# The 512 by 512 channel layer by seven block products, top bits of late weights on another engine, and a new table of the order

## The chip, the cores and the metric

One NeuronCore of one Trainium2 chip runs the whole program as one launch. The metric is device time in microseconds; before the change it is 362.84 us, the median of 3 runs (362.77 to 362.84).

## What is computed

The reference is a retention layer, a spectral mixing layer with a channel layer, and a gated MLP, all in float32. Cut to what matters here:

```python
# retention: B, H, S, D = 2, 8, 768, 64
state = gamma * state + einsum('bhd,bhe->bhde', k[:, :, t], v[:, :, t])
y[:, :, t] = scale * einsum('bhd,bhde->bhe', q[:, :, t], state)
# mixing: d_model = 512
theta = x @ w_theta
y = einsum('ts,bsd->btd', w_tok_r, x * cos(theta)) + einsum('ts,bsd->btd', w_tok_i, x * sin(theta))
u = x + y
x = u + maximum(u @ w_ch, 0.0)
# gated MLP
h = gelu(x @ w_in)                      # 512 -> 1024, halves u and v
v_s = einsum('ts,bsd->btd', w_sg, layernorm(v) * g_ln) + b_sg
out = x + (u * v_s) @ w_out
```

The part in question is `u @ w_ch`: 1536 tokens (2 batches of 768), 512 channels in, 512 out.

## The kernel before

All matrix products are done to float32 precision with three matmuls each. An operand is split into a rounded high half (ScalarE, `split_hi`, line 339) and the rest as a low half (VectorE, `split_lo`, line 345), and `terms3` issues high x high, low x high and high x low. Activations lie with channels on the partitions: `x_tile(g, d)` is channel tile d (of 4) of token group g, 512 tokens wide. Groups 0 and 1 are the first 512 tokens of the two batches, group 2 (`B` in the code) takes the last 256 of both.

The program runs in this order: retention in 12 chunks (`scores`, `outer`, `attend`; masks and decays by VectorE and ScalarE), the angle `theta` of each chunk in two halves, each with its own half of the theta weights, the token mixing (`mix_main` for groups 0 and 1, `mix_rest` for group 2), the channel layer (`channels`, line 902), the up projection (`up_v`, `up_u`, `up_four`), the gate (`gate_tile`) and the last projection (`finish`, `finish_four`). The mixing ends in `mix_main`'s additions, each followed by `split_x`, which makes the high and low halves `uhl` that the channel layer reads.

A layer (`layer`, line 880) for one output tile of one group is 12 matmuls of 128x512: four input tiles, three terms. `seven` does it for four output tiles at a time (two groups, two tiles, all in blocks) with seven block products of 6 matmuls where eight would be the plain way: it needs sums of weight blocks (`sum_weights`) and of token tiles (`sum_tokens`), splits of these sums, and additions behind the products (`both`, and what its callers add). Before the change the up projection's first half (`up_four`) and the last projection (`finish_four`) use it; the channel layer does not.

Weights come as 64-bit words, 1024 to a partition, into one of two raw buffers (`raw`; the theta weights and one more go into x's own memory), and are turned into float32 by three steps: ScalarE rescales the high words (line 411), VectorE shifts the top bits of the low words down (line 421), VectorE joins the two (line 431). Then come a split into halves (lines 339 and 345) and the products.

Every operation is noted in a list first (`plan.op`); the table `ORDER`, a list of operation numbers, then fixes the order in which each engine gets its own, and which buffer each one takes. Loads are issued by SP in that order too; a load that waits for a buffer holds up all that is behind it on SP. Each engine runs its queue in order. PSUM has 8 banks of 512 words.

The lines the change touches: `weight` (line 421), `mix_main` (the splits at line 836), `channels` (902 to 913), `up_four` (1237 to 1251), the loop that calls `channels` (1353 to 1356) and `ORDER`.

```python
def split_x(res, g, d, prio, eng=dve):
    res[g, d] = pair()
    split(res[g, d], lambda: x_tile(g, d), 512, prio, x_keys(g, d), eng)
```

Of the kernel before, what the change touches and what calls it, by code (L numbers as in the profile page):

```python
# [10 lines left out]
F32 = mybir.dt.float32  # L11
F32R = mybir.dt.float32r
I32 = mybir.dt.int32
AF = mybir.ActivationFunctionType
ALU = mybir.AluOpType

B, H, S, D = 2, 8, 768, 64
# [21 lines left out]
RAWS, PAIRS, ONES = 2, 36, 7  # L39

TURNED = (0, 1)


class Buf:
# [21 lines left out]
class Plan:  # L66
# [105 lines left out]


ORDER = [
# [52 lines left out]
]  # L227


# [1 line left out]
def retention_spectral_gmlp(  # L231
# [154 lines left out]
    def weight(k, prio, eng=dve, after=()):  # L386
# [19 lines left out]
        def words(hi):  # L406
# [9 lines left out]
            r=[raw],  # L416
            w=[(raw, 1)],
        )
        dve(
            1024,  # L420
            lambda: V.tensor_scalar(  # L421
                out=words(0), in0=words(0), scalar1=29, scalar2=None, op0=ALU.logical_shift_right
            ),
            fast=True,
            prio=prio,
            r=[raw],
            w=[(raw, 0)],
        )
        dve(
            1024,  # L430
            lambda: V.scalar_tensor_tensor(  # L431
# [379 lines left out]
    def mix_main(b, s, prio):  # L811
# [14 lines left out]
        if s == NCH - 1:  # L826
            for d in range(NP):

                def add(d=d):
                    V.tensor_tensor(  # L830
                        out=x_tile(b, d), in0=ap(y[b, d]), in1=x_tile(b, d), op=ALU.add
                    )

                t = prio + 1 + d * 0.1
                dve(512, add, ps=True, r=[y[b, d]], w=x_keys(b, d), prio=t)
                split_x(uhl, b, d, t + 1 + LATE * (1 - b))

    def mix_rest(b, s, prio):
        i = b * NCH + s
# [59 lines left out]

    x2hl = {}  # L900

    def channels(g, e, prio):

        t = layer(W_CH, uhl, g, e, prio)

        def relu():
            u = x_tile(g, e)
            V.scalar_tensor_tensor(  # L908
                out=u, in0=ap(t), scalar=0.0, in1=u, op0=ALU.max, op1=ALU.add
            )  # L910

        dve(512, relu, ps=True, r=[t], w=x_keys(g, e), prio=prio)
        split_x(x2hl, g, e, prio)

    def gelu(t, o, prio, ps=True):

# [318 lines left out]
        dma(256, put, r=[o], prio=prio)  # L1235

    def up_four(j, ws, ts, prio):
        z, x, y, u, v = seven(W_INU, x2hl, ws, ts, j, prio)
        for g, f, part in ((0, j, z), (1, j, x), (0, 2 + j, y), (1, 2 + j, v)):
            if f % 2 == 0:  # L1240
                gu[g, f], gu[g, f + 1] = halves()
            t = part
            if part is not z:
                t = v if part is v else Buf()
                dve(
                    512,
                    lambda t=t, part=part: V.tensor_tensor(
                        out=ap(t), in0=ap(part), in1=ap(u), op=ALU.add
                    ),
                    ps=part is not v, r=[part, u], w=[t], prio=prio,  # L1250
                )
            gelu(t, gu[g, f], prio, ps=part is z)

    def finish_four(j, ws, ts, prio):
        z, x, y, u, v = seven(W_OUT, ghl, ws, ts, j, prio)
# [94 lines left out]
    for k in range(2):  # L1350
        weight(W_INU + k, t - 10 + 5 * k)
        weight(W_INV + k, t + 30 + 5 * k)
    for g in range(3):
        for e in range(NP):
            channels(g, e, t)
            t += 2.7
    ws = sum_weights(W_INU, t - 8)
    ts = sum_tokens(lambda g, d: (lambda: x_tile(g, d), x_keys(g, d)), t - 4)
    for f in range(NP):
# [144 lines left out]
```

## Time and profile before

| | |
|---|---|
| median of 3 runs | 362.84 us |
| the profiled execution, time | 362.86 us |
| the profiled execution, span | 361.1 us |
| TensorE matmul, busy | 356.1 us (99%), 2308 instructions |
| TensorE weight load, busy | 305.0 us (84%) |
| VectorE, busy | 295.5 us (82%), 476 instructions |
| ScalarE, busy | 187.0 us (52%), 314 instructions |
| GpSimd, busy | 9.0 us (3%) |
| moved by DMA | 44.33 MB |

The span goes from the first to the last instruction; the time of an execution is what the device reports around it. Busy times count from an instruction's start to its end: matmuls overlap each other, and so do the ends and starts of neighbours on VectorE and ScalarE, so that the distance from one start to the next is shorter than a busy time. In the rows PE is TensorE's matmuls, PEld its weight loads, DVE VectorE, ACT ScalarE, SPq the queue on SyncE that issues loads.

### The profile page before, as it was taken

To read this page: it belongs to the slowest core of one execution; us is meant where nothing else is said; L and a number is where in the kernel's file an instruction comes from. 1 tells how busy PE (TensorE), PEld (TensorE's weight loads), DVE (VectorE), ACT (ScalarE), POOL (GpSimd) and SP (SyncE) were. 2 spreads that over 40 slices of the span, in tenths; PEclk is the share of its full clock that TensorE was granted. 3 is DMA by queue.
4 is the path that set the end of the run, shared out by engine and by line. 5 is a ranking of instruction groups with operands and counts; after the bars stand their busy time and mean duration, and the time that the engine had idled before them with its cause. 6 is when DMAs were issued, how large, how long until landed. Compare 5 with 4: busy or idle time off the path is not lost.

```text
span 361.1 us, 5762 instructions
## 1 busy us (share of the span) xinstructions
PE 356.1 (99%) x2308; PEld 305.0 (84%) x2308; DVE 295.5 (82%) x476; ACT 187.0 (52%) x314; POOL 9.0 (3%) x18
## 2 busy tenths in 40 slices
PE   8999999999999999999999999999999999999996
PEld 8878888888999888889988888888888889988885
DVE  2799989899478798952788788799899979989984
ACT  1689895545255458524532365465588651342310
POOL 1110000010001000002000000000000000000000
DMA  7999675435773155056023000011000000000224
GB/s 297 416 408 414 259 238 214 182 116 175 239 269 141 54 193 159 0 218 235 0 118 116 0 2 0 0 30 60 0 0 3 0 1 2 2 0 0 72 104 174
DMA packets 13946, 44.33 MB, mean 123 GB/s; under 512 B 1760, under 2 KB 5344, under 8 KB 11488
## 3 DMA queue, kind: packets, MB, share of 16 engines
q1 hardware_dynamic: 13776, 43.92, 33.2%
q8 instruction: 18, 0.29, 0.3%
q14 instruction: 8, 0.07, 0.1%
q10 hardware_dynamic: 144, 0.05, 0.1%
HBM read 38.19 MB, written 5.77 MB: 122 GB/s over the span
## 4 chain that ended last, share of the span: by engine, by line
PE 93%; DMA 4%; DVE 1%; ACT 1%; issue 0%
PE banks L319 93%; DMA xb<-wts 3%; DMA dec<-decays 1%; DVE xb L431 0%; DVE b L345 0%; ACT xb L411 0%; ACT b L339 0%; PE banks L760 0%; DVE b L1311 0%
## 5 line engine op out<-in xcount | busy, mean ns | idle before, releaser
L319 PE MATMUL banks<-b,b 128*128 128x512 f32 (+2 forms) x1764 | 323.0, 350 | 0.5 <-DVE b L345 0.5
L319 PEld LDWEIGHTS banks<-b,b 128*128 128x128 f32 (+1 forms) x1764 | 274.2, 183 | 47.3 <-issue 1.9
L339 ACT ACTIVATE b<-b 128x512 fp32r<-128x512 f32 (+1 forms) x83 | 63.4, 788 | 72.0 <-PE banks L319 26.4
L345 DVE TENSOR_TENSOR b<-b,b 128x512 fp32r<-128x512 f32 (+1 forms) x83 | 70.8, 873 | 14.4 <-ACT b L339 8.9
L345 DVE TENSOR_TENSOR b<-xa,b 128x512 fp32r<-128x512 f32 (+1 forms) x26 | 18.5, 726 | 10.2 <-ACT b L339 10.2
L339 ACT ACTIVATE b<-xa 128x512 fp32r<-128x512 f32 (+1 forms) x26 | 16.9, 663 | 14.0 <-DVE xa L908 5.6
L511 DVE TENSOR_TENSOR b<-banks,causal 128x512 f32<-128x512 f32 x24 | 16.2, 684 | 7.1 <-PE banks L319 7.1
L411 ACT ACTIVATE b<-b 128x1024 f32<-128x1024 f32 x16 | 18.2, 1149 | 5.0 <-DMA b<-wts 4.9
L431 DVE SCALAR_TENSOR_TENSOR b<-b 128x1024 int32<-128x1024 int32 x16 | 19.7, 1228 | 1.2 <-ACT b L411 0.9
L319 PE MATMUL banks<-b 64*128 64x128 f32 (+1 forms) x352 | 19.4, 256 | 0.2
L319 PEld LDWEIGHTS banks<-b 64*128 64x128 f32 (+1 forms) x352 | 17.3, 165 | 2.2 <-DMA b<-qkv 0.8
L938 ACT ACTIVATE b<-b 128x512 f32<-128x512 f32 x24 | 14.6, 627 | 6.7 <-DVE b L928 6.7
L534 ACT ACTIVATE b<-b,dec 128x64 f32<-128x64 f32 x56 | 14.1, 335 | 6.4 <-DMA b<-qkv 6.4
L920 ACT ACTIVATE b<-banks 128x512 f32<-128x512 f32 x18 | 10.2, 589 | 9.3 <-PE banks L319 9.1
L928 DVE SCALAR_TENSOR_TENSOR b<-b,banks 128x512 f32<-128x512 f32 x18 | 12.1, 678 | 2.1 <-ACT b L920 1.9
L421 DVE TENSOR_SCALAR b<-b 128x1024 int32<-128x1024 int32 x16 | 11.0, 686 | 3.2 <-DMA b<-wts 3.2
L339 ACT ACTIVATE b<-xb 128x512 fp32r<-128x512 f32 (+1 forms) x13 | 8.4, 665 | 9.5 <-DVE xb L866 7.8
L782 DVE TENSOR_TENSOR b<-b,b 128x512 f32<-128x512 f32 x20 | 13.2, 680 | 0.1
L716 ACT ACTIVATE b<-banks 128x512 int32<-128x512 f32 x12 | 7.1, 589 | 11.8 <-PE banks L319 11.8
L1029 ACT ACTIVATE b<-b,rstd 128x512 f32<-128x512 f32 x12 | 9.6, 806 | 5.7 <-DVE rstd L1018 5.7
L944 DVE SCALAR_TENSOR_TENSOR b<-b,banks 128x512 f32<-128x512 f32 x18 | 11.9, 679 | 0.6 <-ACT b L938 0.4
L1202 ACT ACTIVATE b<-banks 128x512 f32<-128x512 f32 x8 | 4.7, 593 | 14.2 <-PE banks L319 13.0
(75 smaller groups left out, 217.6 us busy)
## 6 DMA issues: line engine op xcount, KB each, us to landing
b<-wts SPq DMA_DIRECT2D x16, 1024.0 KB, 5.1
b<-qkv SPq DMA_DIRECT2D x24, 512.0 KB, 9.7
out<-b SPq DMA_DIRECT2D x11, 256.0 KB, 2.1
scr<-b SPq DMA_DIRECT2D x5, 512.0 KB, 4.6
b<-scr SPq DMA_DIRECT2D x20, 128.0 KB, 3.1
b<-wsg SPq DMA_DIRECT2D x9, 256.0 KB, 7.4
xa<-wts SPq DMA_DIRECT2D x2, 1024.0 KB, 11.9
xb<-wts SPq DMA_DIRECT2D x1, 1024.0 KB, 10.6
```

The lines of the kernel that those rows point to most:

```text
L319: nc.tensor.matmul(out=o, lhsT=l, rhs=r, start=start, stop=stop, skip_group_check=more)
L339: act(words, lambda: A.activation(out=hi(), in_=src(), func=AF.Copy), prio=prio, r=r, **k)
L345: lambda: E.tensor_tensor(out=lo(), in0=src(), in1=hi().bitcast(F32), op=ALU.subtract),
L411: lambda: A.activation(out=words(1).bitcast(F32), in_=words(1).bitcast(F32), func=AF.Prelu, scale=REBIAS, alpha=SIGN_UP,),
L421: lambda: V.tensor_scalar(out=words(0), in0=words(0), scalar1=29, scalar2=None, op0=ALU.logical_shift_right),
L431: lambda: V.scalar_tensor_tensor(out=words(0), in0=words(1), scalar=3, in1=words(0), op0=ALU.logical_shift_left, op1=ALU.bitwise_or,),
L511: V.tensor_tensor(out=ap(at[i])[:, h * 512 + lo : h * 512 + hi].rearrange("p (n t) -> p n t", n=n), in0=ap(sc[h])[:, lo:hi].rearrange("p ( ...
L534: A.activation(out=v, in_=v, func=AF.Copy, scale=dk[:, h : h + 1])
L782: V.tensor_tensor(out=v, in0=x, in1=v, op=ALU.mult)
L928: lambda: V.scalar_tensor_tensor(out=ap(s), in0=ap(s), scalar=1.0 / GA, in1=ap(t), op0=ALU.add, op1=ALU.mult),
L938: lambda: A.activation(out=ap(s), in_=ap(s), func=AF.Tanh, scale=GA * GC),
L944: lambda: V.scalar_tensor_tensor(out=ap(o), in0=ap(s), scalar=1.0, in1=ap(t), op0=ALU.add, op1=ALU.mult),
```

## The change

1. The channel layer for groups 0 and 1 goes by `seven` (new `channels_four`, twice) in place of eight calls of `channels`; group 2 keeps its four layers. The additions behind the products are shared with `up_four` (new `sums_of`).
2. `mix_main` no longer splits tiles 0 and 1 of group 1, which the block products don't read.
3. For weights 8 to 18 (all but theta's and the main mixing weights) ScalarE makes the top bits of the low words, in place of VectorE: it reads the top byte of each low word as a number, takes a 32nd of it less 31/64, and writes the rounded whole number.
4. `ORDER` is another table.

```diff
+TOP_BY_ACT = range(W_REST, N_WP)
...
-    48, 50, 62, 49, 63, 105, 51, 106, 0, 52, 168, 118, 64, 53, 119, 55, 54, 56, 6, 67, 58, 57, 66,
+    50, 49, 48, 62, 63, 118, 105, 106, 51, 119, 55, 56, 0, 52, 57, 272, 64, 54, 53, 168, 67, 66, 58,
...
-        dve(
-            1024,
-            lambda: V.tensor_scalar(
-                out=words(0), in0=words(0), scalar1=29, scalar2=None, op0=ALU.logical_shift_right
-            ),
-            fast=True,
...
+        if k in TOP_BY_ACT:
+
+            def top():
+                b = home.bitcast(U8) if keys else ap(raw, I32).bitcast(U8)
+                return b.rearrange("p (n b) -> p n b", b=8)[:, :, 3]
+
+            act(
+                1024,
+                lambda: A.activation(
+                    out=words(0), in_=top(), func=AF.Copy, scale=1 / 32, bias=-31 / 64
+                ),
+                prio=prio, r=[raw], w=[(raw, 0)],
+            )
+        else:
...
-                split_x(uhl, b, d, t + 1 + LATE * (1 - b))
+                if b == 0 or d >= 2:
+                    split_x(uhl, b, d, t + 1 + LATE * (1 - b))
...
+    def channels_four(j, ws, ts, prio):
+        for g, e, t, ps in sums_of(seven(W_CH, uhl, ws, ts, j, prio), j, prio):
+            relu(g, e, t, ps, prio)
+
+    def sums_of(parts, j, prio):
+
+        z, x, y, u, v = parts
+        yield 0, j, z, True
+        for g, e, part in ((1, j, x), (0, 2 + j, y), (1, 2 + j, v)):
+            t = v if part is v else Buf()
+            dve(
+                512,
+                lambda t=t, part=part: V.tensor_tensor(
+                    out=ap(t), in0=ap(part), in1=ap(u), op=ALU.add
+                ),
+                ps=part is not v, r=[part, u], w=[t], prio=prio,
+            )
+            yield g, e, t, False
...
-    for g in range(3):
-        for e in range(NP):
-            channels(g, e, t)
-            t += 2.7
+    ws = sum_weights(W_CH, t - 30)
+    ts = sum_tokens(lambda g, d: (lambda: x_tile(g, d), x_keys(g, d)), t)
+    for j in range(2):
+        channels_four(j, ws, ts, t)
+        t += 9.5
+    for e in range(NP):
+        channels(B, e, t)
+        t += 2.7
```

The new table moves instructions on every engine. First the loads on SP, from the fifth on. Before (L400 is a weight's load: `xb` takes the first theta weight, `xa1` the second; L465 are the q/k/v loads of the chunks, two each; L490 is the query decay table):

```order
L465 DMA b4_111<-qkv 128x1024
L490 DMA dq_86<-qdecays 128x512
L465 DMA b5_114<-qkv 128x1024
L400 DMA xb_90<-wts 128x2048
L465 DMA b8_128<-qkv 128x1024
L465 DMA b9_130<-qkv 128x1024
L465 DMA b13_142<-qkv 128x1024
L400 DMA xa1_89<-wts 128x2048
```

And now, from the fifth on as well (L406 is the weight's load, L485 the q/k/v loads, L510 the decay table):

```order
L485 DMA b4_111<-qkv 128x1024
L485 DMA b5_113<-qkv 128x1024
L485 DMA b6_115<-qkv 128x1024
L510 DMA dq_86<-qdecays 128x512
L485 DMA b7_118<-qkv 128x1024
L406 DMA xb_90<-wts 128x2048
L485 DMA b11_146<-qkv 128x1024
L485 DMA b15_159<-qkv 128x1024
L485 DMA b18_181<-qkv 128x1024
L485 DMA b22_199<-qkv 128x1024
L406 DMA xa1_89<-wts 128x2048
```

Both theta weights stand further back: eight q/k/v loads ahead of the first where there were six, twelve ahead of the second where there were nine.

Second, TensorE ahead of its first theta product. Before, from the second chunk's attend on (64x64 are outer products, 128x128 of one buffer are scores, 64x128 the parts of an attend, L760 the transpose of a chunk, 128x512 theta):

```order
L319 MATMUL banks_65<-b1_105,state1_67 64x128 x8
L319 MATMUL banks_65<-b16_176,b3_109 64x128 x8
L319 MATMUL banks_65<-b5_114 64x64 x8
L760 MATMUL banks_65<-ident_69,xa0_88 128x128 x4
L319 MATMUL banks_65<-b4_111,state0_66 64x128 x8
L319 MATMUL banks_65<-b22_200,b5_114 64x128 x8
L319 MATMUL banks_65<-b8_128 128x128 x8
L319 MATMUL banks_65<-b9_130 128x128 x8
L319 MATMUL banks_65<-b32_273,b23_202 128x512 x2
L319 MATMUL banks_65<-b35_284,b23_202 128x512
```

And now, from the third chunk's attend on:

```order
L325 MATMUL banks_65<-b5_113,state0_66 64x128 x8
L325 MATMUL banks_65<-b27_239,b6_115 64x128 x8
L325 MATMUL banks_65<-b7_118 64x64 x8
L325 MATMUL banks_65<-b4_111,state1_67 64x128 x8
L325 MATMUL banks_65<-b23_201,b7_118 64x128 x8
L325 MATMUL banks_65<-b11_146 128x128 x8
L325 MATMUL banks_65<-b15_159 128x128 x8
L325 MATMUL banks_65<-b18_181 128x128 x8
L325 MATMUL banks_65<-b40_328,b36_314 128x512 x2
L325 MATMUL banks_65<-b44_341,b36_314 128x512
```

The fourth chunk's outer product and attend and two more scores now stand ahead of the first theta product (b40 and b44 are the high and low half of the first theta weight), the transpose behind it; in all 7 scores, 4 outer products and 4 attends, where there were 5, 3 and 3.

Third, VectorE ahead of the first product of the up projection by sums (L927 is the relu, L1199 a token sum for the up projection, L1248 the combining addition behind two products, L351 a low half). The relu that opens the piece waits for the channel layer's last block product but one on TensorE, and the last row is read by the up projection's first product:

```order
L927 SCALAR_TENSOR_TENSOR xa0_88<-banks_65,xa0_88 128x512
L1199 TENSOR_TENSOR b295_2012<-xa0_88,b287_1965 128x512
L1248 TENSOR_TENSOR b290_1979<-banks_65,b290_1979 128x512
L351 TENSOR_TENSOR b280_1940<-b255_1794,b280_1940 128x512
L351 TENSOR_TENSOR b296_2014<-xa0_88,b296_2014 128x512
```

In the kernel before this place has a relu of group 2 and low halves (L908 relu, L345 low half):

```order
L908 SCALAR_TENSOR_TENSOR xb_90<-banks_65,xb_90 128x512
L345 TENSOR_TENSOR b288_2042<-b285_2035,b288_2042 128x512
L345 TENSOR_TENSOR b278_2006<-xa1_89,b278_2006 128x512
L345 TENSOR_TENSOR b296_2083<-b286_2038,b296_2083 128x512
L345 TENSOR_TENSOR b293_2065<-b292_2063,b293_2065 128x512
```

Five instructions stand in both; now two of them are additions that the sums need.

## Rows read from the trace of the kernel before

**Rows 1.** The page, part 1: busy time, share of the span, instructions.
```profile
PE 356.1 (99%) x2308; PEld 305.0 (84%) x2308; DVE 295.5 (82%) x476; ACT 187.0 (52%) x314; POOL 9.0 (3%) x18
```

**Rows 2.** The chain of work that ended last: start, length in us, what.
```profile
0.79 3.97 DMA dec<-decays
...
4.77 10.56 DMA xb<-wts
...
20.34 18.55 PE banks L319 x226
...
39.48 318.51 PE banks L319 x1840
...
358.01 0.42 DVE b L1311
```

**Rows 3.** Waits of PE: line, who was waited for, us, times, longest.
```profile
PE banks L319 <- DVE b L345: 0.5, 1, 0.5
```

**Rows 4.** Groups on PE from 184 to 295 us, shapes apart: count, busy, ns.
```profile
L319 PE MATMUL banks<-b,b 128*128 128x512 f32 x485 | 110.3, 389 | 0.0
L319 PE MATMUL banks<-b,b 128*128 128x256 f32 x12 | 1.6, 283 | 0.0
```

**Rows 5.** Windows: length; busy of PE, PEld, DVE, ACT, POOL; clock, DMA, GB/s.
```profile
5.00:30.00 25.00, 24.32 (x360) 20.53 (x361) 21.04 (x33) 17.46 (x51) 2.82 (x4) 1.00 1.02 414
...
80.00:220.00 140.00, 140.00 (x871) 121.79 (x870) 105.36 (x149) 65.33 (x92) 3.55 (x4) 1.00 0.36 125
220.00:345.00 125.00, 125.00 (x621) 106.48 (x620) 112.98 (x221) 66.57 (x112) 0.00 (x0) 1.00 0.04 13
...
184.00:295.00 111.00, 111.00 (x497) 92.17 (x496) 96.91 (x197) 63.71 (x108) 0.00 (x0) 1.00 0.08 27
```

**Rows 6.** Groups by line and shape on DVE and ACT: count, busy us, mean ns, idle before.
```profile
L345 DVE TENSOR_TENSOR b<-b,b 128x512 fp32r<-128x512 f32 x55 | 36.2, 685 | 2.8 <-ACT b L339 2.8
...
L421 DVE TENSOR_SCALAR b<-b 128x1024 int32<-128x1024 int32 x16 | 11.0, 686 | 3.2 <-DMA b<-wts 3.2
...
L339 ACT ACTIVATE b<-b 128x512 fp32r<-128x512 f32 x55 | 33.2, 627 | 51.5 <-PE banks L319 16.8 <-DVE b L1106 15.4 <-DVE b L1158 9.2
...
L411 ACT ACTIVATE b<-b 128x1024 f32<-128x1024 f32 x16 | 18.2, 1149 | 5.0 <-DMA b<-wts 4.9
```

**Rows 7.** DVE in order of time: start, length in us, what, idle before.
```profile
169.91 0.69 DVE L345 TENSOR_TENSOR b<-xa,b 128x512 fp32r<-128x512 f32 x1 [6.94 <-ACT b L339]
...
201.41 0.68 DVE L1158 TENSOR_TENSOR b<-xa,xa 128x512 f32<-128x512 f32 x1
202.01 0.68 DVE L908 SCALAR_TENSOR_TENSOR xa<-banks,xa 128x512 f32<-128x512 f32 x1
...
216.80 0.69 DVE L908 SCALAR_TENSOR_TENSOR xb<-banks,xb 128x512 f32<-128x512 f32 x1 [1.81 <-PE banks L319]
```

**Rows 8.** PE in order of time, first 31 us: start, length, what (equal names merged).
```profile
7.16 0.94 PE L319 MATMUL banks<-ident 128*128 128x128 f32 x6
8.03 0.69 PE L319 MATMUL banks<-b 128*64 128x64 f32 x16
8.54 1.14 PE L319 MATMUL banks<-b,b 128*64 128x128 f32 x16
9.76 1.78 PE L319 MATMUL banks<-b 64*128 64x128 f32 x32
11.46 1.09 PE L319 MATMUL banks<-b,state 64*64 64x128 f32 x16
...
13.41 0.71 PE L319 MATMUL banks<-b 128*64 128x64 f32 x16
14.05 0.66 PE L760 MATMUL banks<-ident,xa 128*128 128x128 f32 x4
14.64 1.09 PE L319 MATMUL banks<-b,state 64*64 64x128 f32 x16
...
30.65 5.73 PE L319 MATMUL banks<-b,b 128*128 128x512 f32 x24
```

**Rows 9.** ACT in order of time, the second theta weight's first step.
```profile
21.67 1.15 ACT L411 ACTIVATE xa<-xa 128x1024 f32<-128x1024 f32 x1
```

More of the change, by code (lines that the diff above doesn't have):

```diff
@@ L13 @@
 I32 = mybir.dt.int32
+U8 = mybir.dt.uint8
 AF = mybir.ActivationFunctionType
@@ L418, in weight @@
         )
-        dve(
-            1024,
-            lambda: V.tensor_scalar(
-                out=words(0), in0=words(0), scalar1=29, scalar2=None, op0=ALU.logical_shift_right
-            ),
-            fast=True,
[L425 to L428, printed above, removed]
+        if k in TOP_BY_ACT:
[11 more added lines that the diff above has]
+            dve(
+                1024,
+                lambda: V.tensor_scalar(
+                    out=words(0), in0=words(0), scalar1=29, scalar2=None, op0=ALU.logical_shift_right
+                ),
+                fast=True,
+                prio=prio,
+                r=[raw],
+                w=[(raw, 0)],
+            )
         dve(
@@ L900, in retention_spectral_gmlp, with relu @@
     x2hl = {}
-    def channels(g, e, prio):
[L904 to L909, printed above, removed]
-            )
-        dve(512, relu, ps=True, r=[t], w=x_keys(g, e), prio=prio)
-        split_x(x2hl, g, e, prio)
+    def relu(g, e, t, ps, prio):
+        u = x_tile(g, e)
+        dve(
+            512,
+            lambda: V.scalar_tensor_tensor(
+                out=u, in0=ap(t), scalar=0.0, in1=u, op0=ALU.max, op1=ALU.add
+            ),
+            ps=ps, r=[t], w=x_keys(g, e), prio=prio,
+        )
+        split_x(x2hl, g, e, prio)
+    def channels(g, e, prio):
+        relu(g, e, layer(W_CH, uhl, g, e, prio), True, prio)
+    def channels_four(j, ws, ts, prio):
[6 more added lines that the diff above has]
+            t = v if part is v else Buf()
+            dve(
+                512,
+                lambda t=t, part=part: V.tensor_tensor(
+                    out=ap(t), in0=ap(part), in1=ap(u), op=ALU.add
+                ),
+                ps=part is not v, r=[part, u], w=[t], prio=prio,
+            )
+            yield g, e, t, False
     def gelu(t, o, prio, ps=True):
@@ L1237, in up_four @@
     def up_four(j, ws, ts, prio):
-        z, x, y, u, v = seven(W_INU, x2hl, ws, ts, j, prio)
-        for g, f, part in ((0, j, z), (1, j, x), (0, 2 + j, y), (1, 2 + j, v)):
+        for g, f, t, ps in sums_of(seven(W_INU, x2hl, ws, ts, j, prio), j, prio):
             if f % 2 == 0:
                 gu[g, f], gu[g, f + 1] = halves()
[L1242 to L1252, printed above, removed]
+            gelu(t, gu[g, f], prio, ps=ps)
     def finish_four(j, ws, ts, prio):
```

106 rows, old and new, of the table ORDER are left out of this document.

## The prediction

> **What bounds the kernel now.** I read the busy shares first: TensorE is at work for 99% of the span, VectorE 82%, ScalarE 52% [rows 1]. Then the chain of waits [rows 2]: the first load of a theta weight lands at 15.33, its conversion ends at 20.34, and from there TensorE runs unbroken to 357.99; 0.42 us of VectorE and the last store end the span. Then what TensorE waited for [rows 3]: once in the work, 0.5 us, for the low part of that theta weight. So from 20.34 on TensorE has no gap, and whatever leaves its queue leaves the time, unless a wait takes its place. The profiled execution took 362.86 us, 1.76 more than its span; the median of the runs is 362.84, so a sum made against this execution carries over.
>
> **The products.** Eight layers of 12 matmuls (groups 0 and 1, four tiles each) go; two times seven products of 6 come: 96 less 84 is 12 matmuls of 128x512. Their price is the distance from start to start, not the 389 ns that one is in flight. From 184 to 295 us TensorE had no idle, with 485 matmuls of 512 columns and 12 of 256 [rows 4, 5]; the 12 counted as 6, that is 111.0/491 = 0.226 us each. 12 x 0.226 = **2.71 us** off, in the stretch without gaps. Products by sums are in that stretch already (the up projection's), at no other price.
>
> **VectorE and ScalarE.** For the channel layer VectorE gains 4 sums of weights and 8 of tokens, 12 low halves of those, 4 combining and 6 further additions, and loses 2 low halves (group 1's mixed tiles 0 and 1, which no product reads any more): 32 instructions of 512 words. Back to back these start 0.60 us apart (201.41, 202.01 [rows 7]): 19.2 us. It loses 11 top-bit shifts, busy for 686 ns as a 512-word instruction is for 685 [rows 6, 7], so 0.60 apart too: 6.6 us. Net 12.6 us more. ScalarE gains 10 rounded halves and 4 copies of 512 words at 0.63, and 11 top-bit instructions. No row has that form (bytes read eight apart, whole numbers written); nearest is the rescaling of the same words at 1.15 [rows 6], which I take; the ends are 0.63 and twice 1.15. Together 21.4 us, 15.7 to 34 with those ends.
>
> What hides it: from 80 to 220 us, where the channel layer, its weights and its inputs lie, VectorE is idle for 140.0 - 105.4 = 34.6 us and ScalarE for 74.7 [rows 5]. With 12.6 more and a stretch 2.7 shorter, VectorE keeps 19. If that cover were gone, each microsecond would be one on TensorE. The tightest place, by the VectorE rows of the order, is the first product of the up projection: behind the relu that is released by the channel layer's last product but one on TensorE stand, in all, five VectorE instructions (relu, two additions, two low halves), 5 x 0.60 and some 0.4 for handing over, 3.4 us, against one product and one layer on TensorE, 1.36 + 2.71 = 4.07. The kernel before has a queue of five there too (a relu at 216.80 and four low halves [rows 7]), ahead of a product of the same kind, and TensorE did not wait. So: 0. With one more ScalarE step each late weight is ready about 1 us later, and the load that waits for its buffer, with all that is queued behind it on SP, starts as much later; these weights are converted well ahead of their products, and the DMA engines are 36% busy there [rows 5]: 0 again.
>
> **The start.** The new table moves the loads. The first theta weight is issued behind eight q/k/v loads and the decay table, where it stood behind six and the table; the second behind twelve, where it stood behind nine. At 414 GB/s (the stretch from 5 to 30 us [rows 5]) a 512 KB load takes 1.27 us, so they land 2.5 and 3.8 us later: 17.9, and, counted from 21.67, when ScalarE took up the second one [rows 9], 25.5. The first one is converted 5.0 us after landing, as before: 22.9. Ahead of its first product TensorE now has 7 scores, 4 outer products and 4 attends. An outer product takes 0.51 (8.03 to 8.54), with a scores 1.70 (9.76 to 11.46), an attend 1.95, the first one 1.22 [rows 8]: 4 x 1.70 + 3 x 1.2 + 1.2 + 3 x 1.95 = 17.5. It begins when V of chunk 0 has been scaled: decays landed at 4.76 [rows 2], one VectorE instruction and the handing over, 5.7; the wait for the first masks costs some 0.5. So 23.7, behind the weight's 22.9: no idle here, where there was 0.5, and no filling products, where there were 0.87 us of them at 7.16. By 23.7 it has done two scores, an outer product and an attend more than by 20.34, and not yet the transpose (0.59) and two theta products (0.45): 2.4 + 0.5 + 1.95 - 1.04 = 3.8 us of work in 3.36 us. **0.4 us** gained. Ends: 1.4, if all idle and filling time goes; -1.3, if everything lands one load later.
>
> The second theta weight is needed after three products, an attend, an outer product and another product: 23.7 + 4.1 + 1.95 + 0.5 + 1.4 = 31.6. Ready: 25.5 + 5.0, with two other VectorE instructions in between that partly run beside ScalarE, 30.5 to 31.7. I take 0.1 us lost; the ends are 0 and the 4.2 of the second rival.
>
> **Sum:** 362.86 - 2.71 - 0.4 + 0.1 = 359.85; I forecast **359.8 us**.
>
> **Rivals.**
> *VectorE becomes the bound, no gain.* After 220 us it is busy for 113.0 of 125 us [rows 5], and its idle before consists of waits, which more instructions need not fill. If the 24 added instructions that hang on the mixed tiles (32 less the 8 for weight sums; 14.4 us) cannot start before the last of these tiles, they meet the stage from 184 to 220; if a fifth of them is not covered, that costs 2.9: 362.86 - 2.71 + 2.9 = 363.05. Against it: the one long idle, 6.9 us, lies just there, ending at 169.91 [rows 7], and four of the eight token sums need tiles 0 and 2 alone. The Trainium skill speaks for this rival: "Perfetto Trace Analysis", section "Identifying the Most-Contended Engine", says that matmul busy time is no measure of TensorE's headroom and that weight-load busy time should be taken. By that rule TensorE stands at 84%, level with VectorE, and taking out matmuls at VectorE's cost would bring nothing. The trace does not agree here: starts 0.226 us apart fill the 111.0 us without idle, though weight loads are busy for only 92.2 of them.
>
> *The second theta weight is late: slower.* If one more load comes in ahead of it (1.27), it lands at 26.8; if its conversion again takes 9.0 us among other work, as from 21.67 to the first product with it at 30.65 [rows 8, 9], it is ready at 35.8. TensorE then idles 4.2: 362.86 - 2.71 - 0.4 + 4.2 = 363.95. The time is longer than before once that idle exceeds 3.1. For it: VectorE is busy 21.0 of 25 us from 5 to 30 [rows 5], and has more masks to make there now. Against: nothing waited for those 9.0 us, so they were no minimum.
>
> *The change does not take the time out*, because small waits along a new order give it back piece by piece: 361 to 362.1 if up to 2 us of them come together, still faster. For it: VectorE's and ScalarE's queues are cut finer in the new order; against: the order before held 338 us with no wait.
>
> **How the numbers follow.** A measurement of this kernel can tell 0.2%, 0.7 us. The forecast, with the start's ends, 358.8 to 360.9: 0.68. Small waits: 0.15. VectorE, no gain: 0.10. Late weight: 0.07. So faster by over 0.2% has 0.83, the same 0.10, slower 0.07. The range goes from the start's better end, 358.8, to 361.9, in the upper part of the small waits, and leaves some 2 in 10 outside.
>
> **What would show it.** Right: 1104 matmuls of 512 columns, no idle of TensorE behind VectorE from 40 us to the end, its unbroken run from about 23 or 24 to about 355, VectorE some 13 us busier or more, ScalarE some 20, the byte-reading instruction at 1.1 to 1.2 us. Wrong: idle of TensorE behind VectorE at the sums of the channel layer or the up projection (first rival); idle between 31 and 36 us behind the second theta weight (second); many idles of some tenths (third); a product that waits for a weight whose load stood behind a buffer on SP.

## The result, and the profile after

The median of five runs is **359.66 us** (359.16 to 360.20), against 362.84 before: 0.9913 of it, 95% interval 0.9898 to 0.9927, so 3.18 us less. Run again later beside other kernels it took 359.51 us, 0.9910 (0.9897 to 0.9922). The profiled execution took 359.16, the fastest of its five.

The page of the changed kernel, busy time of each engine, answers to [rows 1]:

```profile
PE 352.4 (99%) x2298; PEld 302.7 (85%) x2298; DVE 306.1 (86%) x497; ACT 204.5 (57%) x339; POOL 9.5 (3%) x18
```

VectorE is busy 10.6 us more than before, ScalarE 17.5 more, TensorE 3.7 less. The chain that ended last answers to [rows 2] (start, length in us, what):

```profile
5.35 10.03 DMA b<-qkv
...
15.41 2.02 ACT b L554 x8
...
17.98 0.69 DVE b L351
18.67 0.60 DVE xa L650
19.27 0.61 DVE xb L441
...
22.44 1.24 DVE b L351
...
23.72 18.28 PE banks L325 x200
...
45.77 308.52 PE banks L325 x1762
...
354.31 0.42 DVE b L1341
```

In this chain TensorE's unbroken run begins at 23.72 and ends at 354.29, where it was 20.34 and 357.99. Ahead of it the chain no longer goes through the load of the first theta weight, but through a q/k/v load that landed at 15.38, ScalarE's work on it, and VectorE's queue: the first theta weight's shift (L441) waited behind other work. What TensorE waited for in the work, in all (line, releaser, us, times, longest), answers to [rows 3]:

```profile
PE banks L325 <- DVE b L531: 0.6, 1, 0.6
```

That is the first masks, at 8.6 us. The windows answer to [rows 5], with their columns:

```profile
5.00:30.00 25.00, 24.39 (x363) 21.05 (x361) 20.01 (x32) 14.96 (x41) 1.84 (x3) 1.00 1.02 412
80.00:220.00 140.00, 140.00 (x872) 121.84 (x871) 117.04 (x167) 82.61 (x117) 3.52 (x4) 1.00 0.25 91
184.00:295.00 111.00, 111.00 (x514) 92.92 (x513) 105.02 (x208) 72.97 (x119) 0.00 (x0) 1.00 0.10 38
220.00:345.00 125.00, 125.00 (x621) 106.47 (x620) 115.26 (x225) 67.58 (x113) 0.00 (x0) 1.00 0.08 27
```

From 80 to 345 us TensorE has no idle, as before; VectorE's idle from 80 to 220 went from 34.6 to 23.0 us. The groups of ScalarE by line and shape (count, busy us, mean ns, idle before) show the instruction that no row of before had, beside the one whose price it was given [rows 6]:

```profile
L417 ACT ACTIVATE b<-b 128x1024 f32<-128x1024 f32 x16 | 18.4, 1150 | 0.0
...
L433 ACT ACTIVATE b<-b 128x1024 int32<-128x1024 uint8 x11 | 12.5, 1135 | 0.0
```

And TensorE in order of time answers to [rows 8]:

```profile
3.96 2.01 PE L325 MATMUL banks<-ident 128*128 128x128 f32 x14
5.89 2.68 PE L325 MATMUL banks<-b 128*64 128x64 f32 x48
9.13 1.09 PE L325 MATMUL banks<-b,b 128*64 128x128 f32 x16 [0.56 <-DVE b L531]
...
20.02 2.98 PE L325 MATMUL banks<-b 64*128 64x128 f32 x48
22.93 4.71 PE L325 MATMUL banks<-b,b 128*128 128x512 f32 x18
```

The 14 filling matmuls stand ahead of everything; the first theta product begins at 22.93, and its 18 matmuls took 4.71 us (4.40 in experiment 8, without a wait): the low half of the weight came at 23.68.

### The profile page after: what moved, and what is told of

Same layout as the page of the kernel before. It is cut to its first block, busy times and chain, and to the rows that moved or that the text cites. A ratio compares the mean times of both kernels' runs of the same rounds, so it can differ in the third digit from the quotient of the medians.

```text
span 357.5 us, 5782 instructions
## 1 busy us (share of the span) xinstructions
PE 352.4 (99%) x2298; PEld 302.7 (85%) x2298; DVE 306.1 (86%) x497; ACT 204.5 (57%) x339; POOL 9.5 (3%) x18
## 4 chain that ended last, share of the span: by engine, by line
PE 92%; DMA 4%; DVE 1%; ACT 1%; issue 0%; SPq 0%; DVEq 0%
PE banks L325 92%; DMA b<-qkv 3%; DMA dec<-decays 1%; ACT b L554 1%; DVE b L351 1%; ACT b L345 0%; DVE xb L451 0%; PE banks L780 0%; DVE xb L441 0%; DVE xa L650 0%; DVE b L1341 0%; SPq L510 0%; DVEq L451 0%
## 5 line engine op out<-in xcount | busy, mean ns | idle before, releaser
L345 ACT ACTIVATE b<-b 128x512 fp32r<-128x512 f32 (+1 forms) x95 | 70.7, 766 | 55.0 <-DVE b L1199 16.0
L351 DVE TENSOR_TENSOR b<-b,b 128x512 fp32r<-128x512 f32 (+1 forms) x95 | 78.2, 842 | 4.2 <-ACT b L345 3.7
L345 ACT ACTIVATE b<-xa 128x512 fp32r<-128x512 f32 (+1 forms) x24 | 15.9, 670 | 9.7 <-DVE xa L927 3.6
L345 ACT ACTIVATE b<-xb 128x512 fp32r<-128x512 f32 (+1 forms) x13 | 8.5, 667 | 17.6 <-DVE xb L650 9.9
L351 DVE TENSOR_TENSOR b<-xa,b 128x512 fp32r<-128x512 f32 (+1 forms) x24 | 17.4, 727 | 0.8 <-ACT b L345 0.7
L802 DVE TENSOR_TENSOR b<-b,b 128x512 f32<-128x512 f32 x20 | 13.8, 703 | 4.3 <-ACT b L771 2.6
L1243 ACT ACTIVATE b<-banks 128x512 f32<-128x512 f32 x12 | 7.1, 591 | 10.6 <-PE banks L325 10.6
L961 ACT ACTIVATE b<-banks 128x512 f32<-128x512 f32 x18 | 10.1, 585 | 5.2 <-PE banks L325 4.5
L433 ACT ACTIVATE b<-b 128x1024 int32<-128x1024 uint8 x11 | 12.5, 1135 | 0.0
L850 DVE TENSOR_TENSOR xa<-banks,xa 128x512 f32<-128x512 f32 x8 | 5.5, 687 | 8.0 <-PE banks L325 8.0
L1140 DVE SCALAR_TENSOR_TENSOR b<-banks,gcol,brow 128x512 f32<-128x512 f32 x12 | 9.0, 747 | 3.5 <-PE banks L325 3.5
```

Of the source, the lines that this page charges most:

```text
L345: act(words, lambda: A.activation(out=hi(), in_=src(), func=AF.Copy), prio=prio, r=r, **k)
L351: lambda: E.tensor_tensor(out=lo(), in0=src(), in1=hi().bitcast(F32), op=ALU.subtract),
L433: lambda: A.activation(out=words(0), in_=top(), func=AF.Copy, scale=1 / 32, bias=-31 / 64),
L802: V.tensor_tensor(out=v, in0=x, in1=v, op=ALU.mult)
```

## The experiments

My theory: TensorE has no gap from about 23 us on, so the 12 matmuls are worth their distance, 2.7 us; the work added to VectorE and ScalarE is hidden, with under 1 us to spare at the tightest place; the rest is the start. The rivals were those of the prediction. Each experiment ran in up to 11 executions beside the kernel before, with its ratio against that.

### 1. The start alone

```diff
-    48, 50, 62, 49, 63, 105, 51, 106, 0, 52, 168, 118, ...
+    50, 49, 48, 62, 63, 118, 105, 106, 51, 119, 55, 56, 0, 52, ...
...
```

In the kernel before, the table begins with the changed kernel's first 25 us; in the stretch behind it I moved entries until none of the planned waits that this made was left.

> The kernel before with the start of the changed one: the first 25 us of the order are the change's (the theta weights' loads behind more q/k/v loads, the retention work ahead of theta as in the change), the eight layers and VectorE's top bits stay. Theory (products 2.7, start 0.4): 362.4. If the start is worth what the changed kernel's trace suggests (its time fell by 3.7 in the profiled execution, 2.7 of it for the products): 361.8 to 362.0, and the rest of the change then brings 2.2 to 2.4 on top. Rival (the start gave nothing, the products and small things all): 362.8.

Measured: 362.91 us (362.20 to 363.54), ratio 1.0001 (0.9992 to 1.0010). By itself the new start brought nothing. TensorE in order of time shows why that reading is not the whole of it:

```profile
3.95 2.87 PE L319 MATMUL banks<-ident 128*128 128x128 f32 x14
6.75 2.67 PE L319 MATMUL banks<-b 128*64 128x64 f32 x48
...
23.75 3.02 PE L319 MATMUL banks<-b,b 128*128 128x512 f32 x12
```

The same 14 filling matmuls that took 2.01 us in the changed kernel's profile took 2.87 here, and everything behind them stands 0.8 us later. In every trace such matmuls start 0.213 us apart at first; where they go on long enough, they start 0.112 apart from some moment on: at 4.6 us in the changed kernel's profiled execution, at 6.4 in this one. That moment differs from execution to execution, and experiments 5, 6, 9, 10 and 11 are about it.

### 2. Twelve matmuls more

```diff
+TIMES = {559: 2, 585: 2}
...
-        o.fn()
+        for _ in range(TIMES.get(number[o], 1)):
+            o.fn()
```

The first product of each seven of the channel layer is computed twice into the same bank (the second start overwrites the first).

> The changed kernel with the first product of each seven of the channel layer computed twice: 12 matmuls of 128x512 more, all else the same. Theory (TensorE without gaps bounds): 12 x 0.226 = 2.7 us more, 362.4. Rival (VectorE bounds this stage): VectorE's queue gets 1.36 us of rest twice, so 0 to 0.5 us more, 359.7 to 360.2.

Measured: 362.56 us (361.92 to 362.73), ratio 0.9990 (0.9981 to 0.9999): 2.90 more than the changed kernel's median. The chain of waits gives the price without the start's scatter. The last long piece of this kernel:

```profile
46.02 311.25 PE banks L328 x1774
```

against 308.52 with 1762 in the changed kernel: 12 matmuls, 2.73 us, 0.2275 each. TensorE bounds, VectorE does not. And the kernel with the product count of before and all else changed stands 0.20 us under before by the medians (0.04 to 0.7 by the interval of the ratio): that is what the start and everything other than the products brought.

### 3. Top bits by VectorE

```diff
-TOP_BY_ACT = range(W_REST, N_WP)
+TOP_BY_ACT = ()
```

> The changed kernel with the late weights' top bits by VectorE, as before: 11 shifts at 0.60 for 11 ScalarE instructions at 1.14. Theory (hidden beside TensorE): within 0.3 of the changed kernel, 359.4 to 360.0, VectorE busy 6 to 7.5 us more and ScalarE 12.5 less. Rival (VectorE has nothing left once the sums are added): each shift is 0.6 on TensorE where it falls among the sums, up to 6.6 more, 361 to 366.

Measured: 359.51 us (359.15 to 359.96), ratio 0.9910 (0.9897 to 0.9924): no difference from the changed kernel. Its page:

```profile
PE 352.5 (99%) x2298; PEld 302.8 (85%) x2298; DVE 312.8 (88%) x508; ACT 194.0 (54%) x328; POOL 9.6 (3%) x18
```

VectorE 6.7 us more, ScalarE 10.5 less (I expected 12.5: part of the 1.135 us runs beside a neighbour), and the last long piece of the chain is 308.51 us. So this part of the change is worth nothing by itself in this order, and VectorE at 88% still covers.

### 4. VectorE late at its tightest place

```diff
+TIMES = {648: 3, 635: 3}
```

(the same loop as in experiment 2; 648 is a difference of tokens, 635 a low half, both between a relu and the low half that the up projection's first product waits for).

> The changed kernel with two of VectorE's instructions ahead of the up projection's first product (a difference of tokens and a low half, between the relu at 199.5 and the low half that ends at 202.6) done three times: four instructions more, 2.4 us, in the one place called the tightest. In the changed kernel's trace the product begins 0.8 us after its last low half, and needs that half only from its third matmul, 0.45 later. Theory (slack there is 0.7 to 1.2, nothing else hides it): TensorE idles 1.2 to 1.7 us at 203 us and the time rises by as much, to 360.9 to 361.4. Rival (the 19 us of VectorE's idle hide it): 359.7.

Measured: 360.57 us (360.44 to 361.34), ratio 0.9946 (0.9934 to 0.9959): 0.9 above the changed kernel's median, 1.28 above it in the two profiled executions, whose starts agree (5.89 and 5.90). VectorE and TensorE in order of time, first of the changed kernel, then of this one:

```profile
199.49 0.69 DVE L927 SCALAR_TENSOR_TENSOR xa<-banks,xa 128x512 f32<-128x512 f32 x1 [0.23 <-PE banks L325]
200.09 0.68 DVE L1199 TENSOR_TENSOR b<-xa,b 128x512 f32<-128x512 f32 x1
...
201.89 0.69 DVE L351 TENSOR_TENSOR b<-xa,b 128x512 fp32r<-128x512 f32 x1
```

```profile
199.53 0.69 DVE L930 SCALAR_TENSOR_TENSOR xa<-banks,xa 128x512 f32<-128x512 f32 x1 [0.23 <-PE banks L328]
200.14 2.14 DVE L1202 TENSOR_TENSOR b<-xa,b 128x512 f32<-128x512 f32 x3
...
204.85 0.68 DVE L354 TENSOR_TENSOR b<-xa,b 128x512 fp32r<-128x512 f32 x1
```

```profile
205.58 6.64 PE L328 MATMUL banks<-b,b 128*128 128x512 f32 x28 [0.88 <-DVE b L354]
```

In the changed kernel the queue of five runs from 199.49 to 202.58 and the product begins at 203.37: 0.79 us to spare. The four instructions put the low half at 205.53, 2.95 later. TensorE had by then done five of the product's six matmuls; the sixth, not the third as I had written, is the one that needs this half, and it waited until 205.58. In the changed kernel it stands at 203.37 + 5 x 0.227 = 204.5, so the real room is 1.9 us, and 2.95 less 1.9 is the 1.0 by which the sixth start came late, 1.27 us after the fifth. So the place was named rightly and hides little: the 19 us of VectorE's idle that I counted over the stage don't help here.

### 5. Four filling products in place of seven

```diff
-                keep_warm(idle[0], int((gap - (0.1 if done < 9.0 else 0.5)) / 0.24))
+                keep_warm(idle[0], min(4, int((gap - (0.1 if done < 9.0 else 0.5)) / 0.24)))
```

> The changed kernel with 4 filling products in place of 7 ahead of the first outer product (8 matmuls in the trace, not 14). In the profiles so far TensorE's matmuls of 128x128 go from 0.213 to 0.112 us apart at 4.5 to 6.4 us, another time in each execution, and in the changed order all 14 stand ahead of the first work: it began at 5.89 where the step came at 4.6, and at 6.75 where it came at 6.4. Theory (this wait, up to 0.85 us in some executions, is in the changed kernel's time and makes its runs differ): median 0.2 to 0.6 below the changed kernel's, 359.1 to 359.5, highest less lowest run under 0.6 us. Rival (the runs differ for another reason, and the first outer product waits for its input all the same): 359.6 with the same spread of 1 us; or the clock rises later for lack of work, 360 or more.

Measured: 359.04 us (358.79 to 359.84), ratio 0.9901 (0.9885 to 0.9916). As the theory said for the median, but the spread did not shrink (1.05 us), and experiment 10, the same kernel, takes it back.

### 6. The start alone, four filling products

The edit of experiment 5 in the kernel of experiment 1.

> The first experiment (the kernel before with the start of the changed one) with 4 filling products in place of 7. Theory (the start saves about 0.4 us of idle and filling, which the 14 filling matmuls gave back in the executions where the clock rose late): 362.1 to 362.5, spread under 0.6. Rival (the new start is worth nothing by itself): 362.8 to 363.

Measured: 362.46 us (361.88 to 363.42), ratio 0.9990 (0.9982 to 0.9999): 0.4 us under before, with the theory. Its spread is 1.5 us.

### 7. and 12. The second theta weight one load later

Experiment 7 moves one entry of the table, the second theta weight's load (6), behind a q/k/v load (273), with no filling products after 20 us; experiment 12 has the edit of experiment 5 besides.

```diff
-    ... 121, 70, 6, 110, 71, 109, 273, 108, ...
+    ... 121, 70, 110, 71, 109, 273, 6, 108, ...
...
-            if done < WARM and gap > (0.4 if done < 9.0 else 0.8):
+            if done < 20.0 and gap > (0.4 if done < 9.0 else 0.8):
```

> The changed kernel with the second theta weight's load one q/k/v load later on SP (and no filling products after 20 us). In the changed kernel it landed at 25.6, its low half was made at 31.21, and the first product with it began at 31.57, 0.36 later. Theory (conversion takes what it took, 5.6 us from landing): landing 1.27 later, 26.9, low half at 32.5, TensorE idles 0.4 to 0.9 us at 31.6 to 32.5 and the time rises by as much, to 360.1 to 360.5. Rival (the second one of the prediction: conversion takes 9.0 us once it is late): 4.2 us idle, 363.9. Other rival (the products' high terms and other work cover it): 359.7.

> The seventh experiment (second theta weight one load later) with 4 filling products, so that TensorE comes to that weight at about 29.7 to 30 and not, as in the seventh's profiled execution, 0.7 later than in the changed kernel. Theory: low half at 32.4, needed at 31.2 (or 0.45 later at the third matmul): 0.7 to 1.2 us of idle there and 0.7 to 1.2 above the fifth experiment, 359.8 to 360.3. Rival (late by 4.2): 363. Other rival (covered): 359.1.

Measured: experiment 7 360.35 us (359.59 to 360.91), ratio 0.9927 (0.9915 to 0.9940). That lies in the range forecast, but the wait forecast for it is not in its trace: in its profiled execution the work began at 6.96 and TensorE came to that weight as late as the weight itself. So the trace tells nothing of this wait, and what put the median 0.7 above the changed kernel's is not shown. For experiment 12 it is 359.31 us (359.25 to 359.90), ratio 0.9909 (0.9895 to 0.9923). The trace of experiment 12 is the one to read; VectorE in order of time, first of the changed kernel, then of experiment 12:

```profile
26.31 0.69 DVE L441 TENSOR_SCALAR xa<-xa 128x1024 int32<-128x1024 int32 x1
...
29.98 1.23 DVE L351 TENSOR_TENSOR b<-xa,b 128x1024 fp32r<-128x1024 f32 x1
```

```profile
26.72 0.70 DVE L441 TENSOR_SCALAR xa<-xa 128x1024 int32<-128x1024 int32 x1 [0.88 <-DMA xa<-wts]
...
30.41 1.23 DVE L351 TENSOR_TENSOR b<-xa,b 128x1024 fp32r<-128x1024 f32 x1
```

ScalarE took the weight up at 25.64 and at 26.72, 1.08 later. The low half ended at 31.21 and at 31.64, only 0.43 later: in the changed kernel the shift had waited behind two masks, here VectorE was free. Landing to low half was 5.6 us there and 4.9 here, and TensorE lost 0.1 us at 31.7. My 0.7 to 1.2 missed, because I carried the 5.6 over; the prediction's rival with its 9.0 us is out.

### 8. The first theta weight's bits joined earlier

```diff
-    ... 73, 74, 124, 115, 127, 18, 1, 2, 60, 3, 182, ...
+    ... 73, 74, 124, 1, 2, 3, 115, 127, 18, 60, 182, ...
```

(1 to 3 are that weight's rescaling, shift and joining, 115 the scaling of chunk 2), with the edit of experiment 5.

> The fifth experiment (4 filling products) with the first theta weight's top bits and their joining ahead of the scaling of chunk 2 on VectorE, where they stood behind it. In the changed kernel the low half of that weight came at 23.7, 0.7 after the first product had begun, and TensorE idled 0.2 between its high and its low terms. Theory: that idle goes, 0.2 us below the fifth experiment. Rival (chunk 2 and those behind it come late instead, slack there is 0.75 to 1.25): the same as the fifth experiment or up to 0.5 above.

Measured: 359.09 us (358.84 to 359.71), ratio 0.9897 (0.9884 to 0.9911), the same as experiment 5. Its profile has the gain and a loss. The first 18 theta matmuls take 4.40, without the idle between high and low terms; but at 62.86 TensorE has waited for VectorE (first VectorE in the changed kernel, then VectorE and TensorE here):

```profile
60.63 0.69 DVE L802 TENSOR_TENSOR b<-b,b 128x512 f32<-128x512 f32 x1 [1.45 <-DMA b<-scr]
```

```profile
61.51 0.69 DVE L802 TENSOR_TENSOR b<-b,b 128x512 f32<-128x512 f32 x1 [2.69 <-DMA b<-scr]
62.12 1.88 DVE L650 TENSOR_TENSOR xa<-banks,dq 128x512 f32<-128x512 f32 x3
```

```profile
62.86 3.47 PE L325 MATMUL banks<-b,b 128*128 128x512 f32 x14 [0.61 <-DVE xa L650]
```

L802 needs chunk 2 back from its way through DRAM. That transfer landed 0.88 us later than in the changed kernel (1.53 later than in experiment 5), and behind the wait in VectorE's queue stood the scalings that TensorE needed. The rival's reason, that chunk 2 comes late because it is scaled later, is not what the trace shows: it was scaled 1.6 us later, but it was sent to DRAM (L694) and the last of it asked for again (L700) no later than in the changed kernel. SyncE's queue in order of time, first of the changed kernel, then of this one:

```profile
33.06 0.33 SPq L694 DMA_DIRECT2D scr<-b  x1
...
54.31 0.91 SPq L700 DMA_DIRECT2D b<-scr  x2
```

```profile
32.64 0.33 SPq L694 DMA_DIRECT2D scr<-b  x1
...
54.15 0.96 SPq L700 DMA_DIRECT2D b<-scr  x2
```

The median is in the rival's range. Why the transfer landed late is not shown, nor whether the edit brings it about: the profiled execution, 359.71, is the slowest of its four, and the other three took 358.84 to 359.28.

### 9., 10. and 11. The changed kernel again, and the filling products

Experiment 9 is the changed kernel unaltered, 10 the kernel of experiment 5, 11 the same edit with 2 in place of 4.

> The changed kernel once more, unaltered, on the same chip as the next three, for a direct comparison. Theory (its time moves with the moment at which the filling matmuls get faster): median 359.4 to 359.9, runs between 359.1 and 360.4.

> The fifth experiment (4 filling products in place of 7) once more, on the same chip as the changed kernel. Theory: 358.9 to 359.3, 0.3 to 0.7 below the changed kernel here. Rival (the 0.6 between them came from different chips or executions): no difference above 0.2.

> The changed kernel with 2 filling products in place of 7. TensorE then rests from some 4.8 us to the first outer product at 5.8, whose input is not there earlier. Theory (the fillers only fill): as with 4, 358.9 to 359.4. Rival (without work TensorE's matmuls get faster later): the first scores run at 0.2 us a pair as in the slow part, masks and attends later by 0.5 to 1.5, 359.5 to 360.5.

Measured: experiment 9 359.51 us (359.13 to 359.88); experiment 10 360.05 (358.83 to 361.33), ratio 0.9926 (0.9905 to 0.9946); experiment 11 359.57 (359.18 to 360.31), ratio 0.9914 (0.9901 to 0.9926). TensorE in order of time, of 9, 10 and 11 in turn:

```profile
3.95 3.09 PE L325 MATMUL banks<-ident 128*128 128x128 f32 x14
6.97 2.67 PE L325 MATMUL banks<-b 128*64 128x64 f32 x48
...
23.98 4.38 PE L325 MATMUL banks<-b,b 128*128 128x512 f32 x18
```

```profile
3.96 1.40 PE L325 MATMUL banks<-ident 128*128 128x128 f32 x8
5.61 2.82 PE L325 MATMUL banks<-b 128*64 128x64 f32 x48 [0.25 <-DVE b L549]
...
22.93 1.42 PE L325 MATMUL banks<-b,b 128*128 128x512 f32 x5
```

```profile
3.96 1.06 PE L325 MATMUL banks<-ident 128*128 128x128 f32 x4
5.66 4.29 PE L325 MATMUL banks<-b 128*64 128x64 f32 x48 [0.65 <-DVE b L549]
...
24.02 1.20 PE L325 MATMUL banks<-b,b 128*128 128x512 f32 x4
```

In experiment 9 the filling matmuls stayed 0.213 apart to the last, 6.7 us; work began at 6.97 and the first theta product at 23.98, 1.05 later than in the other execution of the same kernel. Some of that came back at once (the low half was there, no idle between high and low terms), and the profiled time was 359.88 against 359.16. From there on the two executions are alike, the last piece of the chain:

```profile
46.49 308.52 PE banks L325 x1762
```

In experiment 11 the matmuls of the outer products and scores went on at the wide distance until 9.2 us. Its work began at 5.66, before that of the changed kernel, but its first theta product at 24.02, as late as in experiment 9: the rival's course and time. Experiment 10 missed: its median is 0.54 above that of experiment 9 beside it, where the theory had it 0.3 to 0.7 below. Three of its six executions took 360.83 to 361.33; the profiled one was the fastest, so what they lost, and where, is not shown. (A late transfer as in experiment 8 is one candidate.) The ten executions of that kernel have a median of 359.28, the nine of the changed kernel 359.66, with intervals that overlap. I found no version that is shown to beat the changed kernel.

## Why the prediction was right, and where its sizes were off

The forecast was 359.8 us; the time is 359.66.

- **The products**, 2.71 us: measured 2.73 (experiment 2, chain). TensorE had no gap and every matmul counted at its distance. The first rival, VectorE as the bound, is refuted twice: 12 more matmuls cost their full price, and 6.7 us more of VectorE cost nothing. The rule of the Trainium skill that I set against the trace ("Perfetto Trace Analysis", "Identifying the Most-Contended Engine": judge TensorE's headroom by its share of peak arithmetic or by the busy time of its weight loads), taken by the weight loads as the prediction took it, puts VectorE at 86% level with TensorE's 85%; experiments 2 and 3 both contradict it here.
- **VectorE and ScalarE**, 0 us: right. VectorE's 12.6 came out as 10.6, ScalarE's 21.4 as 17.5, since more instructions stand back to back, where each runs partly beside the next (such overlaps add up to 30.9 us on VectorE, 27.5 before, and to 23.9 on ScalarE, 20.6 before); the byte-reading instruction took 1.135 where I had taken 1.15. But what hides the work is the room at each product, not the 19 us that I had left over the stage. At the place I called the tightest the sum gave 4.07 - 3.4 = 0.7 us of room; there were 0.79 to the product's start and 1.9 to the matmul that needs the half.
- **The start**, 0.4 us: not borne out. Experiment 1, with the changed kernel's 14 filling matmuls, gives 0 (between 0.4 more and 0.3 less); only experiment 6, with fewer, gives 0.4 less (0.04 to 0.65). The change as a whole brought 3.18 - 2.73 = 0.45 beyond the products (experiment 2: 0.2, between 0.04 and 0.7), so the total came out near the sum, but not by this term alone: that is in part luck, and a paragraph below the list says what else was in it. Of the term's steps: the weight landed by 17.9 as forecast. It was ready at 23.7, not 22.9, because its shift waited on VectorE (chain). TensorE came to it at 22.93 in one execution and 23.98 in another; the sum said 23.7. In that sum a scores was priced at 1.20; three in a row took 22.93 - 20.02 = 2.91, 0.97 each. So its 17.5 us of work were 16.5 (from 5.89 to 22.93, less the 0.56 of waiting), and the 14 filling matmuls, where the prediction had none, put the beginning of the work, 5.7 in the sum, at 5.89 in one execution and 6.97 in the other.
- **The second theta weight**, 0.1 us: landing was forecast at 25.5 (25.64 taken up), ready at 30.5 to 31.7 (31.21), needed at 31.6 (31.57); it cost nothing. The rival is closed by experiment 12.
- **Small waits**: none behind the first theta product. The stretch behind 46 us is one piece, as in the kernel before.

The profiled execution alone would have misled: it shows 3.70 us, since its filling matmuls got faster early. By the medians 3.2 to 3.4 us lie between experiment 1 or 6 and the changed kernel, 0.5 to 0.7 more than the products. The starts of the single matmuls in the traces show where. From the first theta matmul to the last matmul of the program, experiments 1 and 6 take 334.0 us, experiments 5, 9, 10 and 11 330.7: 3.3 less, of which 2.73 are the products. The other 0.5 falls where a matmul follows one of another shape, 54 times there and 51 times here, and in the step behind that (0.335 us between the first two 128x512 matmuls, where others are 0.227 apart); all other steps between 128x512 matmuls average 0.227 in both. So the order behind the start is worth 0.5 against that of experiments 1 and 6, a term that the sum put at nothing. Against the order of the kernel before, no run parts it from the start.

**What stays open**: the slow executions of experiment 10, the late transfer of experiment 8 and the median of experiment 7.

## What to carry to other kernels

Where one engine runs without a gap, price a removed instruction by its distance from start to start, and added work on the others by the room left at each place where that engine takes up their result; idle summed over a stage says little about it. Count the changes of shape in its queue too: kernels with three more of them took 0.5 us longer here. Where an effect is under 1 us, look first at what differs between two executions of the same kernel, and compare pieces of the chain that begin behind it.

## What the runs showed of the hardware that I had not expected

In every trace matmuls of 128x128 f32 start 0.213 us apart from the beginning. From some moment on they, and the pairs of smaller matmuls, start about half as far apart: from 4.6 us in the changed kernel, 4.75 in experiment 10, 6.4 in experiment 1 and after 6.7 in experiment 9, in all of which TensorE had worked without rest since 1.23, and from 9.2 in experiment 11, where it had rested from 5.0 to 5.66. Two executions of one kernel differ by it. The expectations call this the clock; the profile's rows do not, for they give a granted clock of 1.00, the upper level (2.4 GHz), all through, as in this window of experiment 11 (6 to 9 us, columns as in [rows 5]), in which the matmuls still had the wide distance:

```profile
6.00:9.00 3.00, 3.00 (x36) 2.88 (x34) 0.51 (x2) 0.19 (x1) 0.00 (x0) 1.00 1.00 397
```

The Trainium skill, "TensorE: Matmul & The Clock Gate", section "What's actually happening", says that TensorE begins at the lower level and that the moment of the change varies between executions. The distances, and their scatter, agree with that; the granted clock of the rows does not show it.
